# Splitting first-layer sums from SBUF, an earlier load, and product tiles in turns in a fused conditioned S4D and FFN kernel

## The chip, the cores and the metric

The kernel runs on one core of a Trainium2 chip. The metric is the device time of one execution in microseconds (us). TensorE (PE) multiplies matrices into PSUM, and PEld is its weight load. VectorE (DVE) and ScalarE (ACT) do elementwise work, GpSimd (POOL) and SyncE (SP) mostly issue DMAs here. Each engine runs its own queue of instructions in order and waits on semaphores of the others.

## The reference

```python
mod = (silu(c) @ w_mod)          # sa, ca, ga, sb, cb, gb, each of 576
h = layernorm(x) * (1 + ca) + sa
x = x + ga * S4D(h)              # y = h conv K + h * D_skip, by FFTs
h = layernorm(x) * (1 + cb) + sb
x = x + gb * (relu(h @ w1) @ w2) # 576 -> 4608 -> 576
...
K = 2 * Re(einsum("dn,dnl->dl", C, exp(A dt l)))   # 128 states, l < 2048
```

There are 2048 tokens of 576 channels, all float32.

## The kernel before

The tokens are worked in four blocks of 512. The convolution is done by blocks as well: `conv(s)` transforms the normed input (U) and the kernel (K) of block s (PE into `ps_f`, L757, copied by ACT to Z, L758), finishes the transforms as butterflies on DVE (L509), multiplies spectra on DVE (`product`: outputs Y, scratch T, L509), and transforms back (PE into `ps_i`, L998). The norm before the feed-forward network then makes `xh`, `xl` and `xs`, a high and low part of the normed input (L1059 to L1066). Spectra that later blocks need go to DRAM and back through POOL's DMA queue: saves of U, R and K (Ud, Rd, Kd, L748), loads of them (Ua, R, Ka, L744), and `kt` (L1238), the kernel's time samples.

The convolution kernel K itself is built by `rest`, in pieces `h`: `load` fetches W0, Zr and W2r on POOL (L398 to L400), `rot` turns W by phases on DVE into W1r (L408 to L414), and `products` multiplies W2r and W1r on PE (L440, output `kps`), in four column tiles of 32, `dd`, with 48, 32 or 16 columns by the number of blocks that the piece serves. Each float32 matmul shows as two matmul instructions in the profile. The pieces for block 1, (1, 2, 3) or 1 alone, are done first; those for blocks 2 and 3, 32 columns, are done during block 1 of the feed-forward network.

That network is the main loop, `ffn`: 36 slices of the hidden layer for each block, 144 iterations g in all. `first(g)` sums 14 matmuls of 128x512 into a PSUM tile `hps` (L1305; two buffers). ACT takes `hh` = relu of it, rounded to the high part (L1310), and DVE takes the low part `hl` from `hps` and `hh` (L1311). `second(g - 2)`, 14 more matmuls, adds into five accumulators (L1330), which ACT evacuates at a block's end (L1416; `oT` and `o`). In each iteration the weights are split as well: ACT rounds `w` (L1276 and L1283), DVE subtracts (L509, `w<-r,w`).

The rest of the work is written as Python generators that `yield` a cost (DVE work in us), `None` for a small PE piece, or -1 for a break. `step(g)` is called four times in an iteration and pulls pieces from the generator of the block, until a rate, a room or a -1 stops it. During block 0 the generator is first `rest` for block 1's pieces and then `conv(1)`; during block 1 it is `finish(0)`, `rest` for blocks 2 and 3, and `conv(2)`; and so on. A scheduler orders each engine's queue from that program order; some instructions are held to it (`kept`).

Of the kernel before, what the change touches and what calls it, by code (L numbers as in the profile page):

```python
# [10 lines left out]
F32 = mybir.dt.float32  # L11
F32R = mybir.dt.float32r
I32 = mybir.dt.int32
AF = mybir.ActivationFunctionType
# [32 lines left out]
class KGen:  # L47
# [335 lines left out]
    def rest(self, psum, items, beside=iter(())):  # L383


        nc, k = self.nc, self.k
        v = nc.vector.tensor_tensor
        kes, rows = {}, {}
        most = 16 * max(len(blocks) for _, blocks in items)
        with ExitStack() as ctx:  # L390
            pt = k.pool(ctx, f"kr{items[0][1][0]}")

            def load(h):
                W2 = pt.tile([P, 2, 32, H], F32, tag="W2", bufs=2, name=f"W2r_{h}")
                W0 = pt.tile([P, 16, 2, H], F32, tag="W0", bufs=2 if most == 48 else 1, name=f"W0_{h}")
                Z = pt.tile([P, 2, 2, H], F32, tag="Z", bufs=2, name=f"Zr_{h}")
                d = nc.gpsimd.dma_start
                d(out=W0.rearrange("p (y a) r c -> p y (a r c)", y=2), in_=strips(k.W1d[h], 2))  # L398
                d(out=Z.rearrange("p i r c -> p (i r c)"), in_=k.Zd[h])
                k.gate = d(out=W2.rearrange("p r (y b) c -> p (r y) (b c)", y=2), in_=strips(k.W2d[h], 4))  # L400
                return W2, W0, Z

            def rot(out, X, Z, i):
                cb = [P, 32, H]
                flat = "p a r c -> p (a r) c"
                T = pt.tile([P, 16, 2, H], F32, tag="T", name="T")
                zr, zi = (Z[:, i, r].unsqueeze(1).broadcast_to(cb) for r in range(2))
                v(T.rearrange(flat), X.rearrange(flat), zi, op=ALU.mult)  # L408
                yield 1.75
                v(out.rearrange(flat), X.rearrange(flat), zr, op=ALU.mult)  # L410
                yield 1.75
                v(out[:, :, 0], out[:, :, 0], T[:, :, 1], op=ALU.subtract)  # L412
                yield 0.95
                v(out[:, :, 1], out[:, :, 1], T[:, :, 0], op=ALU.add)  # L414
                yield 0.95

            def rots(W1, W0, Z, blocks):
                a = [W1[:, 16 * i : 16 * i + 16] for i in range(len(blocks))]
                if blocks[0] == 1:
                    yield from rot(a[0], W0, Z, 0)  # L420
                    if len(blocks) > 1:
                        yield from rot(a[1], W0, Z, 1)
                        yield from rot(a[2], a[0], Z, 1)
                else:
                    yield from rot(a[0], W0, Z, 1)
                    yield from rot(a[1], a[0], Z, 0)

            def products(h, W1, W2, blocks):
                na = 16 * len(blocks)
                key = (h // 6, blocks)  # L430
                if key not in kes:
                    kes[key] = pt.tile([P, na, 72], F32, name=f"ker_{h}")
                ke = kes[key]
                for half in range(2):
                    ps = psum.tile([P, 6, na], F32, tag="cps", bufs=1, name="kps")
                    for q in range(6):
                        for dd in range(4):
                            ch = dd * 12 + 6 * half + q
                            for r in range(2):
                                nc.tensor.matmul(  # L440
                                    ps[32 * dd : 32 * dd + 32, q, :],
                                    W2[:, r, :, ch],
                                    W1[:, :na, r, ch],
                                    start=(r == 0),
                                    stop=(r == 1),
                                )
                        if q == 2:
                            yield None
                    q0 = 12 * (h % 6) + 6 * half
                    nc.scalar.activation(  # L450
                        ke[:, :, q0 : q0 + 6], ps.rearrange("p q a -> p a q"), AF.Copy
                    )
                    yield None
                rows[key] = rows.get(key, 0) + 1
                if rows[key] == 6:
                    yield -1
                    for i, s in enumerate(blocks):
                        self.store(
                            s, h // 6, ke[:, 16 * i : 16 * i + 16].rearrange("p a q -> p (a q)"),
                            nc.gpsimd,  # L460
                        )

            nxt = load(items[0][0])
            yield -1
            prev = iter(())
            for i, (h, blocks) in enumerate(items):
                W2, W0, Z = nxt
                W1 = pt.tile([P, most, 2, H], F32, tag="W1", bufs=2, name=f"W1r_{h}")
                yield from spread(rots(W1, W0, Z, blocks), prev, len(blocks))
                if i + 1 < len(items):  # L470
                    nxt = load(items[i + 1][0])
                prev = products(h, W1, W2, blocks)
                if i + 2 == len(items):
                    yield next(beside, -1)
            yield from both(prev, beside)
# [11 lines left out]
class Body:  # L487
# [317 lines left out]

    def norms(self, st, kept):

        nc = self.nc
        rs = []
        for i in range(4):  # L810
            mv = self.sm.tile([P, 5], F32, tag="mv", bufs=4, name="mv")
            nc.vector.bn_aggr(out=mv[:, 0:2], in_=st[i])
            sq = nc.scalar.activation(mv[:, 2:3], mv[:, 1:2], AF.Sqrt, bias=self.eps)
            if kept:
                self.tc.keep_in_program_order(sq)
            else:
                self.kept(sq)
            rs.append(mv)
        for mv in rs:
            nc.vector.reciprocal(mv[:, 3:4], mv[:, 2:3])  # L820
            nc.vector.tensor_scalar(
                mv[:, 4:5], mv[:, 0:1], mv[:, 3:4], -1.0, op0=ALU.mult, op1=ALU.mult
            )
        return rs

    def sums(self, name):
        return [self.sm.tile([P, 2, 6], F32, tag="st", bufs=8, name=name) for _ in range(4)]
# [11 lines left out]
    def norm1(self, x2, h):  # L839

        f = self.nc.vector.scalar_tensor_tensor
        st = self.sums("st1")
        for p in range(2):
            yield from self.stats(
                lambda i: x2[:, i, p * PC : (p + 1) * PC], [t[:, p] for t in st]
            )
        rs = self.norms(st, False)
        yield 2.0
        for i in range(4):
            mv = rs[i]  # L850
            f(h[:, i], x2[:, i], mv[:, 0:1], self.m["ca"], op0=ALU.subtract, op1=ALU.mult)
            f(h[:, i], h[:, i], mv[:, 3:4], self.m["sa"], op0=ALU.mult, op1=ALU.add)
            yield 1.6

    def conv(self, s):
# [33 lines left out]
        def spec_K(p, Z):  # L889
            R = self.load(self.Rd[s - 1][p], "R")  # L890
            Rs.append(R)
            K = self.spec(f"K_{s}_{p}")
            yield from self.butterfly(Z, K, -1)
            yield -1
            if s + 1 < NB:
                self.save(self.Rd[s][p], K)
            f = nc.vector.scalar_tensor_tensor
            K2 = self.spec(f"K2_{s}_{p}")
            f(K2[:, :, 0], R[:, :, 1], self.sgn[:, 1:2], K[:, :, 0], op0=ALU.mult, op1=ALU.add)
            yield 1.35  # L900
            f(K2[:, :, 1], R[:, :, 0], self.sgn[:, 0:1], K[:, :, 1], op0=ALU.mult, op1=ALU.add)
            yield 1.35
            yield -1
            if s + 1 < NB:
                self.save(self.Kd[s][p], K2)
            Ks.append(K2)

        def product(p, Y):
            def pair(t):
                if t == 0 or s == 1:  # L910
                    Ka = (Rs if t else Ks)[p]
                else:
                    Ka = self.load(self.Kd[s - t][p], "Ka")
                Ua = Us[p] if t == s else self.load(self.Ud[t][p], "Ua")
                return Ka, Ua

            order = [0, s, *range(1, s)]
# [14 lines left out]
            yield from self.butterfly(Y, V, 1)  # L932
            Vs.append(V)

        Us, Ks, Rs, Vs = [], [], [], []
        if s == 1:
            ZU = self.spec("Z")
            yield from mm_U(0, ZU)
# [3 lines left out]
            yield from both(spec_U(1, Z1), mm_K(0, ZK))  # L942
            kt[1] = self.load_kt(s, 1)
            yield from spec_K(0, ZK)
            ZK = self.spec("Z")
            Y = self.spec(f"Y_{s}_0")
            yield from both(product(0, Y), mm_K(1, ZK))
        else:
            ZK = self.spec("Z")
            yield from both(self.norm1(x2, h), mm_K(0, ZK))  # L950
# [295 lines left out]
    def ffn(self, gens):  # L1246
# [50 lines left out]
        def first(g):  # L1297
# [9 lines left out]
                    step(g)  # L1307
            hh = ff.tile([P, 512], F32R, tag="hh", bufs=3, name="hh")
            hl = ff.tile([P, 512], F32R, tag="hl", bufs=3, name="hl")
            nc.scalar.activation(hh, ps, AF.Relu)  # L1310
            nc.vector.scalar_tensor_tensor(hl, ps, 0.0, hh, op0=ALU.max, op1=ALU.subtract)  # L1311
            return hh, hl

        def second(g, hh, hl):
# [246 lines left out]
```

## Time and profile before

| | |
|---|---|
| time, median of 3 runs | 1366.92 us (1363.95 to 1371.61) |
| profiled execution, span | 1360.4 us |
| PE busy | 1226.0 us, 90% |
| DVE busy | 871.4 us, 64% |
| ACT busy | 503.5 us, 37% |
| POOL busy | 195.3 us, 14% |

For the profiled execution only the span of its records is known; it lies 6.5 us under the median of the timed runs. Start times in the profile are counted from the start of that span. Feed-forward work begins at about 213 us; block 0 ends near 551, block 1 lasts from 559 to 849, block 2 to 1110, and block 3 to 1342. A row of a timeline has start, duration, engine, line, operation, output and inputs, shape, and in brackets the idle time before it and what ended that.

### The profile page before, as it was taken

What the parts mean: (1) busy time and instruction counts of PE and PEld (TensorE: products, weight loads), DVE (VectorE), ACT (ScalarE), POOL (GpSimd) and SP (SyncE); (2) the same over time, 40 slices, a digit from 0 to 9 for tenths busy, and PEclk for the clock granted to TensorE, in tenths of its full rate; (3) what the DMA queues carried; (4) which work ended last, traced back from release to release, by engine and by line L of the source; (5) the groups of instructions that cost most, each with busy time, mean ns of one, the idle gap of its engine ahead of it and who ended that gap; (6) DMA issues with size and microseconds to landing.
All of it is one profiled execution on the core that took longest, in us unless ns stands there. A gap on an engine that the chain in (4) does not pass through costs nothing.

```text
span 1360.4 us, 26053 instructions
## 1 busy us (share of the span) xinstructions
PE 1226.0 (90%) x10608; PEld 973.7 (72%) x10608; DVE 871.4 (64%) x1351; ACT 503.5 (37%) x1014; POOL 195.3 (14%) x271
## 2 busy tenths in 40 slices
PE   5125797999999987999999999999999999999998
PEld 3124565777787766777777887787888888888886
DVE  5978997998878698469737986266999222111111
ACT  7986234222224311622233225333322253233321
POOL 1777231111120100021101100100010000000000
PEclk9557899999999998999999999999999999999999
DMA  6666499988898755699689894677997567666651
GB/s 196 243 246 241 135 356 366 331 292 275 292 344 289 265 199 207 205 362 316 236 278 342 294 362 143 206 245 233 317 348 259 178 177 211 198 195 197 197 174 61
DMA packets 132424, 340.47 MB, mean 250 GB/s; under 512 B 22352, under 2 KB 22672, under 8 KB 132304
## 3 DMA queue, kind: packets, MB, share of 16 engines
q1 hardware_dynamic: 105200, 215.21, 48.9%
q0 software_dynamic: 26816, 123.01, 24.6%
q8 instruction: 83, 1.36, 0.4%
q10 hardware_dynamic: 288, 0.59, 0.1%
q14 instruction: 37, 0.30, 0.1%
HBM read 258.55 MB, written 80.22 MB: 249 GB/s over the span
## 4 chain that ended last, share of the span: by engine, by line
PE 70%; DVE 11%; DMA 10%; issue 4%; ACT 2%; POOL 1%; SPq 0%; DVEq 0%; ACTq 0%; POOLq 0%
PE acc L1330 28%; PE hps L1305 28%; PE kps L440 5%; PE ps_f L757 4%; PE kps L262 3%; DVE T L509 2%; DVE Y L509 2%; DMA Ua<-Ud 2%; DMA Ud<-U 2%; DVE k L133 1%; PE ps_i L998 1%; DMA h<-in_x_dram 1%; DMA Ka<-Rd 1%; DMA Zr<-Zd 1%; DMA W1d<-W 1%
## 5 line engine op out<-in xcount | busy, mean ns | idle before, releaser
L1330 PE MATMUL acc<-hh,w 128*128 128x512 f32 x1296 | 422.1, 400 | 0.3 <-DVE w L509 0.3
L1305 PE MATMUL hps<-xh,w 128*128 128x512 f32 x1152 | 394.3, 402 | 4.4 <-ACT xh L1061 3.5
L1311 DVE SCALAR_TENSOR_TENSOR hl<-hps,hh 128x512 fp32r<-128x512 f32 x144 | 99.0, 688 | 291.3 <-ACT hh L1310 291.0
L1330 PEld LDWEIGHTS acc<-hh,w 128*128 128x128 f32 x1296 | 242.1, 188 | 52.5 <-DVE w L509 0.9
L1330 PE MATMUL acc<-hl,w 128*128 128x512 f32 x720 | 278.7, 399 | 0.0
L1305 PEld LDWEIGHTS hps<-xh,w 128*128 128x128 f32 x1152 | 217.4, 190 | 52.1 <-ACT xh L1061 4.7
L1305 PE MATMUL hps<-xl,w 128*128 128x512 f32 x576 | 230.8, 401 | 0.2 <-DVE xl L1066 0.2
L1310 ACT ACTIVATE hh<-hps 128x512 fp32r<-128x512 f32 x144 | 86.0, 598 | 354.6 <-PE hps L1305 347.0
L1283 ACT ACTIVATE w<-r 128x576 fp32r<-128x576 f32 x144 | 98.6, 686 | 217.9 <-issue 168.4
L1330 PEld LDWEIGHTS acc<-hl,w 128*128 128x128 f32 x720 | 135.3, 188 | 28.2
L1305 PEld LDWEIGHTS hps<-xl,w 128*128 128x128 f32 x576 | 109.2, 190 | 24.8 <-DVE xl L1066 1.5
L1305 PE MATMUL hps<-xs,w 128*128 128x512 f32 x288 | 97.2, 417 | 14.3 <-DVE hl L1311 14.0
L1276 ACT ACTIVATE w<-r 128x640 fp32r<-128x640 f32 x142 | 104.0, 733 | 12.4 <-DMA r<-in_w_dram 12.4
L262 PE MATMUL kps<-W,W 128*32 128x16 f32 x2304 | 40.3, 215 | 71.5 <-POOL W L59 47.3
L262 PEld LDWEIGHTS kps<-W,W 128*32 128x32 f32 x2304 | 37.9, 150 | 76.2 <-POOL W L59 49.7
L440 PEld LDWEIGHTS kps<-W1r,W2r 128*32 128x32 f32 x3456 | 68.4, 146 | 30.7 <-issue 16.8
L509 DVE TENSOR_TENSOR Y<-Y,T 128x1152 f32<-128x1152 f32 x64 | 84.7, 1351 | 0.2
L440 PE MATMUL kps<-W1r,W2r 128*32 128x48 f32 (+2 forms) x3456 | 77.4, 238 | 7.0 <-DVE W1r L412 3.3
L1305 PEld LDWEIGHTS hps<-xs,w 128*128 128x128 f32 x288 | 52.8, 190 | 28.3 <-DVE hl L1311 17.1
L758 ACT ACTIVATE Z<-ps_f 128x288 f32<-128x288 f32 x104 | 42.4, 407 | 63.1 <-PE ps_f L757 62.3
L509 DVE TENSOR_TENSOR w<-r,w 128x512 fp32r<-128x512 f32 (+2 forms) x108 | 57.9, 572 | 8.6 <-ACT w L1283 8.6
L509 DVE TENSOR_TENSOR W<-Z 128x576 f32<-128x576 f32 x52 | 37.1, 752 | 29.3 <-ACT Z L758 29.3
(216 smaller groups left out, 1362.8 us busy)
## 6 DMA issues: line engine op xcount, KB each, us to landing
r<-in_w_dram SPq DMA_DIRECT2D x144, 320.0 KB, 4.2
r<-in_w_dram SPq DMA_DIRECT2D x144, 288.0 KB, 3.7
w<-L1d SPq DMA_DIRECT2D x108, 320.0 KB, 3.0
w<-L2d SPq DMA_DIRECT2D x108, 288.0 KB, 3.2
W2r<-W2d POOLq DMA_DIRECT2D x18, 1536.0 KB, 9.4
W2d<-W SPq DMA_DIRECT2D x10, 1536.0 KB, 7.4
W<-W1d POOLq DMA_DIRECT2D x18, 768.0 KB, 8.9
Ua<-Ud POOLq DMA_DIRECT2D x12, 1152.0 KB, 10.3
```

The lines of the kernel that those rows point to most:

```text
L133: self.nc.vector.scalar_tensor_tensor(f[:, i].rearrange(pair, u=2), th, float(slot), k[:, i].rearrange(pair, u=2), op0=ALU.mult, op1=ALU.s ...
L262: self.nc.tensor.matmul(ps[32 * dd : 32 * dd + 32, 12 * u + q, :], W2[:, r, :, ch], W1[:, u, :, r, ch], start=(r == 0), stop=(r == 1),)
L440: nc.tensor.matmul(ps[32 * dd : 32 * dd + 32, q, :], W2[:, r, :, ch], W1[:, :na, r, ch], start=(r == 0), stop=(r == 1),)
L509: return self.kept(self.nc.vector.tensor_tensor(*args, **kw))
L757: kept(nc.tensor.matmul(o, fc[:, n2, c, :], src(n2), start=True, stop=True))
L758: nc.scalar.activation(Z[:, n2, c], ps[:, :PC], AF.Copy)
L1276: nc.scalar.activation(w[:, 0], r, AF.Copy)
L1283: nc.scalar.activation(w[:, 0:D], r2[g], AF.Copy)
L1305: nc.tensor.matmul(ps, a, x, start=(i == 0), stop=(i == 13))
L1310: nc.scalar.activation(hh, ps, AF.Relu)
L1311: nc.vector.scalar_tensor_tensor(hl, ps, 0.0, hh, op0=ALU.max, op1=ALU.subtract)
L1330: nc.tensor.matmul(acc[i], a, x, start=(f == 0 and j in (0, 3, 6, 9, 12)), stop=(f == NF - 1 and j in (2, 5, 8, 11, 13)),)
```

## The change

1. `first`: ACT writes the relu of `hps` to a new float32 tile `raw` in SBUF; ACT copies `raw` to `hh`; DVE subtracts `raw - hh`. Only ACT's first operation reads `hps`.
2. `norms` is cut into `roots` and `factors`; the norm ahead of a convolution breaks off for three steps between them.
3. In `conv(1)` the load of Ua is issued between the two halves of K's butterfly, not in `product`; Y gets its buffer before Z, and the second half's transform of K begins three pieces later.
4. `rest` for blocks 2 and 3 breaks off five times in place of once after its first load.
5. In `products` the loop over real and imaginary part, r, stands outside that over the column tile, dd: consecutive matmuls go to different tiles.
6. The memory for DMA descriptors is set to 8192 bytes.

```diff
-                        for dd in range(4):
-                            ch = dd * 12 + 6 * half + q
-                            for r in range(2):
+                        for r in range(2):
+                            for dd in range(4):
+                                ch = dd * 12 + 6 * half + q
                                 nc.tensor.matmul(
...
             nxt = load(items[0][0])
-            yield -1
+            for _ in range(1 if most == 48 else 5):
+                yield -1
...
-        rs = self.norms(st, False)
-        yield 2.0
+        rs = self.roots(st, False)
+        yield 1.0
+        for _ in range(3):
+            yield -1
+        self.factors(rs)
+        yield 1.0
...
             K = self.spec(f"K_{s}_{p}")
-            yield from self.butterfly(Z, K, -1)
+            W = self.spec("W")
+            yield from self.butterfly1(Z, W)
+            if s == 1:
+                Uas.append(self.load(self.Ud[0][p], "Ua"))
+            yield from self.butterfly2(W, K, -1)
...
+            Y = self.spec(f"Y_{s}_0")
             ZK = self.spec("Z")
-            Y = self.spec(f"Y_{s}_0")
-            yield from both(product(0, Y), mm_K(1, ZK))
+            yield from both(product(0, Y), after(3, mm_K(1, ZK)))
...
-            nc.scalar.activation(hh, ps, AF.Relu)
-            nc.vector.scalar_tensor_tensor(hl, ps, 0.0, hh, op0=ALU.max, op1=ALU.subtract)
+            raw = ff.tile([P, 512], F32, tag="raw", bufs=2, name="raw")
+            nc.scalar.activation(raw, ps, AF.Relu)
+            nc.scalar.activation(hh, raw, AF.Copy)
+            nc.vector.tensor_tensor(hl, raw, hh, op=ALU.subtract)
...
-    nc = bacc.Bacc("TRN2", target_bir_lowering=False, num_devices=1)
+    nc = bacc.Bacc("TRN2", target_bir_lowering=False, num_devices=1, dynamic_dma_scratch_size=8192)
```

The added lines shift later ones: L744 and L748 become L745 and L749, L1238 becomes L1259, L1305 becomes L1326, L1310 becomes L1332 (`raw`) and L1333 (`hh`), L1311 becomes L1334, L1330 becomes L1353, L1416 becomes L1439.

How the order of instructions changes is shown at three places. The first is POOL's queue in `conv(1)`, before (a DMA's tile has its number; Ud_0_101 and Ud_1_102 are block 0's spectra, the two halves):

```order
L748 DMA Ud_0_103<-U_0_5378 128x4x576
L744 DMA R<-Rd_0_109 128x4x576
L748 DMA Ud_1_104<-U_1_5469 128x4x576
L1238 DMA kt<-kd_1_60 128x16x72
L748 DMA Rd_0_111<-K_0_5563 128x4x576
L748 DMA Kd_0_115<-K_1_0_5615 128x4x576
L744 DMA Ua<-Ud_0_101 128x4x576
L744 DMA R<-Rd_1_110 128x4x576
L748 DMA Rd_1_112<-K_1_5846 128x4x576
L744 DMA Ua<-Ud_1_102 128x4x576
```

And after:

```order
L749 DMA Ud_0_103<-U_0_5436 128x4x576
L745 DMA R<-Rd_0_109 128x4x576
L749 DMA Ud_1_104<-U_1_5542 128x4x576
L745 DMA Ua<-Ud_0_101 128x4x576
L1259 DMA kt<-kd_1_60 128x16x72
L749 DMA Rd_0_111<-K_0_5645 128x4x576
L749 DMA Kd_0_115<-K_1_0_5694 128x4x576
L745 DMA R<-Rd_1_110 128x4x576
L745 DMA Ua<-Ud_1_102 128x4x576
L749 DMA Rd_1_112<-K_1_5923 128x4x576
```

The first Ua moves ahead of kt, Rd and Kd, the second ahead of one Rd.

The second place is the change from block 0 to block 1. On PE, before (acc_0 are block 0's accumulators; xs_6182 and xh_6180 are block 1's input):

```order
L1330 MATMUL acc_0_3035<-hh,w_6324 128x512 x2
L1330 MATMUL acc_0_3035<-hl,w_6324 128x512
L1305 MATMUL hps<-xs_6182,w_6162 128x512 x2
L1305 MATMUL hps<-xs_6182,w_6262 128x512 x2
L1330 MATMUL acc_0_3036<-hh,w_6324 128x512
L1049 MATMUL ps_t<-ident,h_0_6241 128x128 x2
L1049 MATMUL ps_t<-ident,h_1_6242 128x128 x2
L1330 MATMUL acc_0_3036<-hh,w_6324 128x512
```

And after:

```order
L1353 MATMUL acc_0_3044<-hh,w_6385 128x512 x2
L1353 MATMUL acc_0_3044<-hl,w_6385 128x512
L1353 MATMUL acc_0_3045<-hh,w_6385 128x512
L1353 MATMUL acc_0_3045<-hl,w_6385 128x512
L1326 MATMUL hps<-xs_6257,w_6223 128x512 x2
L1326 MATMUL hps<-xs_6257,w_6322 128x512 x2
L1070 MATMUL ps_t<-ident,h_0_6324 128x128 x2
L1070 MATMUL ps_t<-ident,h_1_6325 128x128 x2
```

Block 0's last sums now all stand ahead of block 1's first matmul. On ACT at the same place, before:

```order
L1059 ACTIVATE xf<-ps_t,m_sb,m_cb 128x512
L1416 ACTIVATE oT<-acc_0_3035,m_gb 128x512
L1061 ACTIVATE xh_6180<-xf 128x512
L1059 ACTIVATE xf<-ps_t,m_sb,m_cb 128x512
L1416 ACTIVATE oT<-acc_0_3036,m_gb 128x512
L1061 ACTIVATE xh_6180<-xf 128x512
L1059 ACTIVATE xf<-ps_t,m_sb,m_cb 128x512
L1061 ACTIVATE xh_6180<-xf 128x512
L1059 ACTIVATE xf<-ps_t,m_sb,m_cb 128x512
L1061 ACTIVATE xh_6180<-xf 128x512
L1310 ACTIVATE hh<-hps 128x512
L1276 ACTIVATE w_6392<-r_6364 128x640
```

And after:

```order
L1439 ACTIVATE o_6528<-acc_0_3045,m_gb 128x512
L1082 ACTIVATE xh_6255<-xf 128x512
L1080 ACTIVATE xf<-ps_t,m_sb,m_cb 128x512
L1304 ACTIVATE w_6546<-r_6438 128x576
L1082 ACTIVATE xh_6255<-xf 128x512
L1080 ACTIVATE xf<-ps_t,m_sb,m_cb 128x512
L1082 ACTIVATE xh_6255<-xf 128x512
L1332 ACTIVATE raw<-hps 128x512
L1297 ACTIVATE w_6466<-r_6436 128x640
L1333 ACTIVATE hh<-raw 128x512
L1332 ACTIVATE raw<-hps 128x512
L1297 ACTIVATE w_6511<-r_6482 128x640
```

The evacuations of the accumulators all stand ahead of the third xh now (the four oT just above these rows), and a weight split stands between `raw` and `hh`.

The third place is the first piece of `rest` in block 1. On PE before, the products follow the sums of block 1's sixth slice (weights w_6503):

```order
L1305 MATMUL hps<-xl_6181,w_6503 128x512
L1305 MATMUL hps<-xh_6180,w_6503 128x512
L440 MATMUL kps<-W1r_6585,W2r_6566 32x32
L1330 MATMUL acc_36_6515<-hh,w_6550 128x512 x2
L1330 MATMUL acc_36_6515<-hl,w_6550 128x512
L440 MATMUL kps<-W1r_6585,W2r_6566 32x32 x47
```

And after, behind those of the seventh (w_6663):

```order
L1326 MATMUL hps<-xl_6256,w_6663 128x512
L1326 MATMUL hps<-xh_6255,w_6663 128x512
L440 MATMUL kps<-W1r_6710,W2r_6644 32x32 x48
L1353 MATMUL acc_36_6593<-hh,w_6683 128x512 x2
L1353 MATMUL acc_36_6593<-hl,w_6683 128x512
```

The products stand one iteration later against the sums; on DVE the rotations that make W1r follow the same number of `hl`s (40) as before.

More of the change, by code (lines that the diff above doesn't have):

```diff
@@ L806, in norms, with roots @@
     def norms(self, st, kept):
+        rs = self.roots(st, kept)
+        self.factors(rs)
+        return rs
+    def roots(self, st, kept):
         nc = self.nc
@@ L818, in norms, with factors @@
             rs.append(mv)
+        return rs
+    def factors(self, rs):
+        nc = self.nc
         for mv in rs:
@@ L823, in norms @@
             )
-        return rs
     def sums(self, name):
@@ L846, in norm1 @@
             )
-        rs = self.norms(st, False)
-        yield 2.0
+        rs = self.roots(st, False)
+        yield 1.0
+        for _ in range(3):
+            yield -1
+        self.factors(rs)
+        yield 1.0
         for i in range(4):
@@ L913, in pair @@
                     Ka = self.load(self.Kd[s - t][p], "Ka")
-                Ua = Us[p] if t == s else self.load(self.Ud[t][p], "Ua")
+                if t == s:
+                    return Ka, Us[p]
+                Ua = Uas[p] if s == 1 else self.load(self.Ud[t][p], "Ua")
                 return Ka, Ua
@@ L933, in back @@
             Vs.append(V)
-        Us, Ks, Rs, Vs = [], [], [], []
+        Us, Ks, Rs, Vs, Uas = [], [], [], [], []
         if s == 1:
```

## The prediction

> **What bounds the kernel now.** I read the page first, then the stage table, the waits, and the timelines of the stages in which TensorE (PE) is not full. The page's first section and its chain:
>
> ```profile
> PE 1226.0 (90%) x10608; PEld 973.7 (72%) x10608; DVE 871.4 (64%) x1351; ACT 503.5 (37%) x1014; POOL 195.3 (14%) x271
> ...
> PE 70%; DVE 11%; DMA 10%; issue 4%; ACT 2%; POOL 1%; SPq 0%; DVEq 0%; ACTq 0%; POOLq 0%
> ```
>
> PE is the bound on average, but DVE and DMA hold a fifth of the chain. The stage table (span from : to, its length, then busy time per engine) says where:
>
> ```profile
> core 0: us, PE busy (x) PEld busy (x) DVE busy (x) ACT busy (x) POOL busy (x), PEclk, DMA share, GB/s
> ...
> 245.00:345.00 100.00, 97.93 (x1741) 78.04 (x1731) 94.22 (x100) 23.51 (x44) 14.09 (x21) 1.00 0.85 297
> 345.00:483.00 138.00, 136.29 (x1306) 105.43 (x1305) 107.21 (x156) 44.93 (x91) 18.59 (x27) 1.00 0.80 279
> 483.00:541.00 58.00, 45.29 (x174) 34.69 (x173) 55.11 (x79) 9.70 (x16) 3.00 (x4) 0.92 0.64 223
> 541.00:594.00 53.00, 53.00 (x247) 41.54 (x247) 23.69 (x52) 27.32 (x48) 6.20 (x10) 0.99 0.74 249
> 594.00:603.00 9.00, 5.72 (x109) 4.37 (x108) 6.41 (x7) 1.57 (x3) 1.31 (x2) 0.84 1.03 394
> 603.00:852.00 249.00, 245.21 (x2018) 193.56 (x2018) 186.23 (x239) 85.11 (x159) 25.30 (x34) 1.00 0.82 284
> ```
>
> From 483 to 541 PE idles 12.7 us and the granted clock is 0.92, which is 58 x 0.08 = 4.6 us more; DVE is busy 55.11 of 58, so DVE sets the pace there. From 594 to 603 there are 3.3 us of idle and 9 x 0.16 = 1.4 us of clock. Elsewhere after 245 PE is at least 97% busy. The PE timeline shows what it waits for (in brackets the idle time before, and its releaser):
>
> ```profile
> 524.95 1.22 PE L1305 MATMUL hps<-xs,w 128*128 128x512 f32 x2 [4.81 <-DVE hl L1311]
> ...
> 536.04 1.22 PE L1305 MATMUL hps<-xs,w 128*128 128x512 f32 x2 [2.81 <-DVE hl L1311]
> ...
> 598.50 0.31 PE L440 MATMUL kps<-W1r,W2r 128*32 128x32 f32 x2 [3.28 <-DVE W1r L412]
> ```
>
> First-layer sums wait for `hl`, because both `hps` buffers are full until DVE has read them, and DVE's queue is late. Why DVE is late, and (second fence) what POOL does before that:
>
> ```profile
> 466.45 2.63 DVE L509 TENSOR_TENSOR Y<-K,Ua 128x1152 f32<-128x1152 f32 x2 [5.01 <-DMA Ua<-Ud]
> ...
> 512.05 2.63 DVE L509 TENSOR_TENSOR Y<-K,Ua 128x1152 f32<-128x1152 f32 x2 [2.79 <-DMA Ua<-Ud]
> ```
>
> ```profile
> 440.73 0.76 POOL L748 DMA_DIRECT2D Ud<-U  x1 [8.96 <-DVE U L509]
> ...
> 454.82 0.76 POOL L748 DMA_DIRECT2D Kd<-K  x1 [2.49 <-DVE K L901]
> 455.57 0.75 POOL L744 DMA_DIRECT2D Ua<-Ud  x1
> ...
> 501.06 0.75 POOL L744 DMA_DIRECT2D Ua<-Ud  x1
> ```
>
> Each Ua is issued behind the saves of K's results and lands 10.9 us later (455.57 to 466.45), while DVE stands idle for 5.01 and 2.79 us.
>
> **The change, part by part.**
>
> *Ua behind the butterfly's first half.* The first Ua now stands right behind the save of Ud on POOL, so it can be issued near 441.5 and land near 452.5, 14 us ahead of its use; the three DMAs moved behind it (kt, Rd, Kd) go 0.75 us later each, and each of them waits longer for its producer than that. The second stands ahead of Rd and Kd but waits for the buffer of the half before; it is issued perhaps 5 us sooner. Both waits go: 5.01 + 2.79 = 7.8 us off DVE's queue, which sets the end of this stage. I take 7.8. The lower end is 3 (only the later Ua is near the stalls, and the queue of DVE has other waits); the upper is 14, when the freed `hps` lets PE hold one more first layer ahead as well (14 matmuls, 3.2 us at 0.23 us each, the step between two rows at 547 below) and the lost clock returns. Late next is DVE's own work.
>
> *Sums split from SBUF.* The rows for the three forms, and for the same kind of split from SBUF in the norm:
>
> ```profile
> L1310 ACT ACTIVATE hh<-hps 128x512 fp32r<-128x512 f32 x144 | 86.0, 598 | 354.6 <-PE hps L1305 347.0 <-DVE x L509 4.7 <-DVE Y L509 2.4
> ...
> L1311 DVE SCALAR_TENSOR_TENSOR hl<-hps,hh 128x512 fp32r<-128x512 f32 x144 | 99.0, 688 | 291.3 <-ACT hh L1310 291.0
> ...
> L1061 ACT ACTIVATE xh<-xf 128x512 fp32r<-128x512 f32 x16 | 10.1, 631 | 5.0 <-DMA W1d<-W 4.3 <-DVE xf L1057 0.3
> ...
> L1066 DVE TENSOR_TENSOR xl<-xf,xh 128x512 fp32r<-128x512 f32 x16 | 11.1, 692 | 19.0 <-ACT xh L1061 18.9
> ```
>
> ACT gets 144 x 0.631 = 91 us more, 37% becoming 44%; DVE's `hl` costs the same (692 against 688 ns). `hps` comes free after ACT's `raw`, not after DVE: that is what removes the `hl` stalls of PE. `hh` comes 0.63 us later, or about 1.3 with the weight split that the order puts between; `second` uses it two iterations (about 12 us) later, so in steady state this costs nothing, the cover being that distance. The place without cover is the start of block 1:
>
> ```profile
> 547.07 0.39 PE L1305 MATMUL hps<-xl,w 128*128 128x512 f32 x1
> 547.30 0.40 PE L1305 MATMUL hps<-xh,w 128*128 128x512 f32 x1
> 547.53 1.13 PE L998 MATMUL ps_i<-V,gc 128*128 128x288 f32 x4
> ...
> 558.74 1.07 PE L1305 MATMUL hps<-xs,w 128*128 128x512 f32 x4
> ```
>
> ```profile
> 557.84 0.69 DVE L1064 TENSOR_TENSOR xs<-xf,xs 64x512 fp32r<-64x512 f32 x1 [1.21 <-ACT xs L1061]
> ```
>
> ```profile
> L1416 ACT ACTIVATE oT<-acc,m_gb 128x512 f32<-128x512 f32 x12 | 7.5, 690 | 0.0
> ```
>
> The first matmul of block 1 (558.74) starts as xs is ready (558.53), with 17 acc matmuls left behind it as filler. Now these stand ahead, and ACT evacuates all five accumulators among xf, xs and xh, where two stood before: three more of about 0.69 us, 2.1, and 0.6 for hh: I take a loss of 2.5 (1 to 8; 8 if PE also sits out the 9.9 us from the last ps_i, 548.66, to xs with 33 matmuls, 7.6 us, to do meanwhile, and waits for each xh, with clock lost on top).
>
> The Trainium skill ("VectorE: DVE Perf Modes", section "Rules for kernel authors") advises, for elementwise work on a matmul's output, to accept the PSUM source or to copy to SBUF first only where many operations follow; here one follows, which speaks against this edit. The rows agree that the operation itself gains nothing (692 against 688 ns), but the rule does not count when the PSUM buffer is given back. By it alone the edit only lengthens the way to `hl`, and what that gives here is rival 1's result, with its chance.
>
> *Products four steps on.* PE's products of block 1 stand one iteration (28 matmuls, 6.3 us) later, while the rotations on DVE keep their place among the `hl`s. That covers the 3.28 us and most of the clock behind it: 4.5 of 3.3 + 1.4 (0 to 4.7; 0 if DVE's rotations slip as far). DVE's wait for Zr stays beside PE:
>
> ```profile
> 588.22 1.76 DVE L408 TENSOR_TENSOR T<-W,Zr 128x1536 f32<-128x1536 f32 x1 [4.34 <-DMA Zr<-Zd]
> ```
>
> *Product tiles in turns.* 3456 small matmuls, on one column tile four in a row now; the nearest rows:
>
> ```profile
> 189.52 0.75 PE L632 MATMUL mps_sb<-wm_sb,cb 128*32 128x128 f32 x20
> ...
> 247.75 2.33 PE L440 MATMUL kps<-W1r,W2r 128*32 128x48 f32 x96
> ...
> 252.93 1.64 PE L440 MATMUL kps<-W1r,W2r 128*32 128x16 f32 x94
> ...
> 638.54 0.95 PE L440 MATMUL kps<-W1r,W2r 128*32 128x32 f32 x48
> ```
>
> Start to start, taking off one duration (266, 212 and 235 ns by the grouped rows): 48 columns (2330 - 266) / 95 = 21.7 ns, 16 columns 15.4, 32 columns 15.2. L632 already goes over its tiles in turns, and does 128 columns in (750 - 276) / 19 = 24.9 ns, hardly more than 48 on one tile: turns do overlap. Bounds: nothing at one end; at the other, all scale as L632 does (128 columns on one tile would be 58 by the 48-column rate, so a factor 0.43): 21.7 to 9.3 and 15.3 to 6.6. Between, I take 15.4 for 48 columns, a rate that the rows show, and 2 ns off the others. 48 columns: 1152 x 6.3 = 7.3 us, but most of them lie from 245 to 345, where DVE has only 5.8 us to spare; I take 4. The others, in stages where PE is full: by the table of L440's own rows
>
> ```profile
> 345.00:483.00 138.00, 19.20 (x816) 16.95 (x816) 1.00 0.80 279
> ...
> 603.00:852.00 249.00, 20.93 (x1056) 18.44 (x1056) 1.00 0.82 284
> ```
>
> (816 + 1056) x 2 ns = 3.7. Together 7.5 (0 to 5.8 + 1872 x 8.7 ns = 22).
>
> The Trainium skill ("TensorEngine Tiling (Array Packing)", section "Instruction Overhead") gives each matmul some 60 cycles, so that few columns cost the same as 60: by that alone turns bring nothing, which is rival 3's result. The rows speak against it as a floor for every instruction: 48 and 16 columns differ, 21.7 against 15.4 ns. No run here shows the floor in turns yet.
>
> *Norm factors behind the roots.*
>
> ```profile
> 407.11 0.54 DVE L820 RECIPROCAL mv<-mv 128x1 f32<-128x1 f32 x3 [5.46 <-ACT mv L813]
> ```
>
> DVE stops waiting 5.46 us for the roots, but in that stage PE is busy 136.29 of 138: 0, hidden by PE (up to 1.7). *Smaller scratch for DMA descriptors*: few POOL transfers are in flight together: 0, no row can price it.
>
> **The sum.** 7.8 - 2.5 + 4.5 + 7.5 = 17.3 us off the span of 1360.4, so 1343.1. The median of the runs, 1366.9, lies 6.5 above the profiled span, and what lies around the span does not change: 1366.9 - 17.3 = 1349.6, in round numbers 1350.
>
> **Rivals.** (1) Slower: `hl` stands at the head of DVE's queue while `hh` is now 1.3 us later, and where DVE is the pace that is lost each time. In the stages where DVE is over 90% busy, 245 to 345 and 483 to 541, and in as much again of the start and of 426 to 483, some 18 iterations are so placed: 23 us, with the Ua gain gone and 12 from turns and products kept: 1366.9 + 23 - 12 = 1378. It decides if DVE reaches `hl` less than 1.3 us behind the sums, as it did here:
>
> ```profile
> 456.27 0.69 DVE L1311 SCALAR_TENSOR_TENSOR hl<-hps,hh 128x512 fp32r<-128x512 f32 x1 [0.27 <-ACT hh L1310]
> ```
>
> Against it: sums that are no longer held by `hl` come earlier against DVE's queue. 8%.
> (2) The Ua gain is eaten at block 1's start, since xs and the xh are one chain through ACT: loss 8 instead of 2.5, and turns bring half: 1349.6 + 5.5 + 3.75 = 1359. 17%. (3) The turns bring nothing, a fixed cost per matmul: 1357. 13%. (4) The turns reach L632's factor for all: 22 instead of 7.5, 1335. 15%. The forecast itself 47%.
>
> A measurement of this kernel tells about 0.5%, 6.8 us, from no change. Faster by more (under 1360.1) holds the forecast, (3), (4) and half of (2): 0.78 with some kept for what is not listed; same 0.14; slower 0.08. The range reaches from (4) to a little beyond (2): 1334 to 1364.
>
> **What would show it.** In the changed trace no `Y<-K,Ua` waits for Ua, and PE's idle time between 470 and 541 falls from about 13 to below 5 us with a clock of 1.0; `hl` releases no PE matmul any more. At block 1's start PE idles some 2 to 3 us at xs or xh. The 3.28 us before L440 are gone. Runs of 96 products with 48 columns take about 1.75 us in place of 2.33. If `hl` waits for `hh` where DVE is full, rival 1; if the idle at xs is above 6 us, rival 2; if 2.33 stays, rival 3. The forecast is wrong in sign only if the longer way to `hh` holds up DVE's queue.

## The result, and the profile after

The changed kernel takes 1350.91 us (median of 6 runs, 1348.6 to 1353.41) against 1367.59 for the kernel before in the same runs: ratio 0.9896, 95% interval 0.987 to 0.9923, so some 14 us (11 to 18). The forecast was 1350, that is 17.3 us less. The time came out; several terms of the sum did not, and they are what can be learned from. The two profiled executions, from which everything below is read, differ by 11.1 us (spans 1360.4 and 1349.3).

The page of the changed kernel, first section and chain:

```profile
span 1349.3 us, 26128 instructions
...
PE 1219.7 (90%) x10608; PEld 970.2 (72%) x10608; DVE 870.7 (65%) x1351; ACT 579.4 (43%) x1158; POOL 195.2 (14%) x271
...
PE 72%; DVE 11%; DMA 8%; issue 4%; ACT 3%; POOL 1%; SPq 0%; DVEq 0%; POOLq 0%; ACTq 0%
```

ACT is busy for 76 us more, DVE for as long as before, and DMA has less of the chain. The stage table, cut within 0.4 us of the first matmul of each block's first layer:

```profile
214.00:543.50 329.50, 317.55 (x3418) 249.43 (x3416) 291.19 (x391) 121.85 (x229) 41.00 (x60) 0.98 0.84 297
543.50:834.50 291.00, 284.08 (x2278) 224.09 (x2278) 204.13 (x262) 116.81 (x218) 32.79 (x46) 0.99 0.81 285
834.50:1102.00 267.50, 263.70 (x1157) 210.98 (x1156) 166.11 (x233) 118.33 (x213) 14.60 (x20) 0.99 0.71 241
```

and the same of the kernel before:

```profile
212.60:558.70 346.10, 324.26 (x3405) 251.90 (x3406) 291.03 (x390) 100.41 (x190) 40.98 (x60) 0.98 0.80 280
558.70:852.50 293.80, 286.73 (x2297) 226.15 (x2297) 207.42 (x265) 103.64 (x190) 32.81 (x46) 0.99 0.82 285
852.50:1113.00 260.50, 260.45 (x1148) 209.72 (x1147) 163.12 (x229) 95.95 (x171) 14.57 (x20) 1.00 0.76 247
```

Block 0 is 17 us shorter, block 1 is 3 us shorter, and block 2 is 7 us longer, which nothing in the prediction said. Block 0 first. In its last stretch this is all that DVE waited for before (from 456 us to the `xs` of block 1; each line has the total in us, how often, and the longest):

```profile
DVE Y L509 <- DMA Ua<-Ud: 7.8, 2, 5.0
DVE hl L1311 <- ACT hh L1310: 4.5, 2, 4.2
DVE x L509 <- PE ps_i L998: 3.2, 2, 3.1
DVE w L509 <- ACT w L1283: 2.9, 1, 2.9
DVE xs L1064 <- ACT xs L1061: 1.2, 1, 1.2
```

and after (from 455 us to the same point):

```profile
DVE xs L1085 <- ACT xs L1082: 5.1, 1, 5.1
DVE x L510 <- PE ps_i L1019: 0.2, 1, 0.2
```

19.6 us of waiting became 5.3: 14.3 us, and the stretch from the `hl` at 456.3 (455.4 after) to xs went from 101.6 to 87.4 us. The two differences agree, so the waits explain the stretch; only the one for `xs` grew. Ua lands in time, as the POOL and DVE timelines of the changed kernel show:

```profile
440.91 0.76 POOL L745 DMA_DIRECT2D Ua<-Ud  x1
...
482.47 0.75 POOL L745 DMA_DIRECT2D Ua<-Ud  x1 [4.50 <-DVE W L510]
```

```profile
456.01 2.63 DVE L510 TENSOR_TENSOR Y<-K,Ua 128x1152 f32<-128x1152 f32 x2
...
499.17 1.35 DVE L510 TENSOR_TENSOR Y<-K,Ua 128x1152 f32<-128x1152 f32 x1
```

No bracket stands behind the two products, so neither waited. The stage in which PE idled 12.7 us before, at a granted clock of 0.92 (483 to 541), is now

```profile
483.00:534.00 51.00, 48.53 (x207) 38.48 (x206) 50.72 (x81) 16.19 (x27) 1.74 (x3) 1.00 0.71 249
```

with 2.5 us of idle time and a clock of 1.00. No sum waits for `hl` there any more; the stalls that are left are for the weights' low part, which DVE makes as well:

```profile
518.38 1.82 PE L1353 MATMUL acc<-hh,w 128*128 128x512 f32 x5 [1.29 <-DVE w L510]
...
527.21 1.82 PE L1353 MATMUL acc<-hh,w 128*128 128x512 f32 x5 [0.98 <-DVE w L510]
```

Now block 2. PE's one long wait there, and ACT and DVE before it:

```profile
875.48 0.75 PE L758 MATMUL ps_f<-kt,fcK 128*128 128x288 f32 x2 [3.79 <-ACT Z L759]
```

```profile
869.77 0.41 ACT L759 ACTIVATE Z<-ps_f 128x288 f32<-128x288 f32 x1 [0.84 <-PE ps_f L758]
874.28 0.85 ACT L820 ACTIVATE mv<-mv,eps 128x1 f32<-128x1 f32 x4 [4.10 <-DVE mv L819]
875.04 0.39 ACT L759 ACTIVATE Z<-ps_f 128x288 f32<-128x288 f32 x1
```

```profile
871.16 2.98 DVE L804 BATCH_NORM_STATS2 st<-x 128x6 f32<-128x288 f32 x8 [6.84 <-DMA x<-in_x_dram]
```

The roots of the norm for block 3 stand in ACT's queue while x, its input, is still under way; the copy of `ps_f` behind them waits, and PE, out of buffers, waits for that copy. Before, ACT waited for the same roots (3.0 us), but one Z copy stood behind them where two stand now (first the order before, then after):

```
L758 ACTIVATE Z<-ps_f 128x288 x3
L813 ACTIVATE mv<-mv,eps 128x1 x4
L758 ACTIVATE Z<-ps_f 128x288
```

```
L759 ACTIVATE Z<-ps_f 128x288 x3
L820 ACTIVATE mv<-mv,eps 128x1 x4
L759 ACTIVATE Z<-ps_f 128x288 x2
```

### The profile page after: what moved, and what is told of

Same layout as the page of the kernel before. It is cut to its first block, busy times and chain, and to the rows that moved or that the text cites. A ratio compares the mean times of both kernels' runs of the same rounds, so it can differ in the third digit from the quotient of the medians.

```text
span 1349.3 us, 26128 instructions
## 1 busy us (share of the span) xinstructions
PE 1219.7 (90%) x10608; PEld 970.2 (72%) x10608; DVE 870.7 (65%) x1351; ACT 579.4 (43%) x1158; POOL 195.2 (14%) x271
## 4 chain that ended last, share of the span: by engine, by line
PE 72%; DVE 11%; DMA 8%; issue 4%; ACT 3%; POOL 1%; SPq 0%; DVEq 0%; POOLq 0%; ACTq 0%
PE hps L1326 29%; PE acc L1353 29%; PE kps L440 5%; PE ps_f L758 4%; PE kps L262 3%; DVE T L510 2%; DVE Y L510 1%; DMA Ud<-U 1%; DMA x<-in_x_dram 1%; PE ps_i L1019 1%; DVE k L133 1%; DMA r<-in_w_dram 1%; DMA Zr<-Zd 1%; DVE W L510 1%; DMA W1d<-W 1%
## 5 line engine op out<-in xcount | busy, mean ns | idle before, releaser
L1353 PE MATMUL acc<-hh,w 128*128 128x512 f32 x1296 | 425.7, 400 | 2.5 <-DVE w L510 2.3
L1326 PE MATMUL hps<-xh,w 128*128 128x512 f32 x1152 | 394.3, 402 | 2.8 <-ACT xh L1082 2.8
L1334 DVE TENSOR_TENSOR hl<-raw,hh 128x512 fp32r<-128x512 f32 x144 | 99.4, 690 | 290.7 <-ACT hh L1333 287.9
L1353 PE MATMUL acc<-hl,w 128*128 128x512 f32 x720 | 284.3, 401 | 0.0
L1353 PEld LDWEIGHTS acc<-hh,w 128*128 128x128 f32 x1296 | 243.9, 189 | 55.3 <-DVE w L510 4.0
L1326 PEld LDWEIGHTS hps<-xh,w 128*128 128x128 f32 x1152 | 216.6, 189 | 50.4 <-ACT xh L1082 4.2
L1326 PE MATMUL hps<-xl,w 128*128 128x512 f32 x576 | 230.6, 400 | 0.1
L1332 ACT ACTIVATE raw<-hps 128x512 f32<-128x512 f32 x144 | 86.1, 598 | 322.4 <-PE hps L1326 316.2
L1353 PEld LDWEIGHTS acc<-hl,w 128*128 128x128 f32 x720 | 136.1, 189 | 28.5
L1326 PEld LDWEIGHTS hps<-xl,w 128*128 128x128 f32 x576 | 109.0, 189 | 25.0 <-DVE xl L1087 1.9
L1326 PE MATMUL hps<-xs,w 128*128 128x512 f32 x288 | 99.4, 413 | 0.3 <-DVE xs L1085 0.3
L1333 ACT ACTIVATE hh<-raw 128x512 fp32r<-128x512 f32 x144 | 89.7, 623 | 0.3
L440 PEld LDWEIGHTS kps<-W1r,W2r 128*32 128x32 f32 x3456 | 64.1, 146 | 31.0 <-issue 19.5
L440 PE MATMUL kps<-W1r,W2r 128*32 128x48 f32 (+2 forms) x3456 | 72.3, 238 | 9.3 <-issue 5.9
L1326 PEld LDWEIGHTS hps<-xs,w 128*128 128x128 f32 x288 | 53.6, 190 | 12.6 <-DVE xs L1085 0.9
```

Source lines behind the costliest of these rows:

```text
L440: nc.tensor.matmul(ps[32 * dd : 32 * dd + 32, q, :], W2[:, r, :, ch], W1[:, :na, r, ch], start=(r == 0), stop=(r == 1),)
L1326: nc.tensor.matmul(ps, a, x, start=(i == 0), stop=(i == 13))
L1332: nc.scalar.activation(raw, ps, AF.Relu)
L1333: nc.scalar.activation(hh, raw, AF.Copy)
L1334: nc.vector.tensor_tensor(hl, raw, hh, op=ALU.subtract)
L1353: nc.tensor.matmul(acc[i], a, x, start=(f == 0 and j in (0, 3, 6, 9, 12)), stop=(f == NF - 1 and j in (2, 5, 8, 11, 13)),)
```

## The experiments

After the first trace the theory was that DVE's queue sets the end of block 0, with Ua its main wait (theory 1); the rival was that the `hps` buffers, freed late, set it, so that the split alone would do (rival 2). The stage lengths below, in us, are of one profiled execution each, between the first matmuls of the first layers. They scatter: the changed kernel and "conv(3) later" have the same order on PE in blocks 0 and 1, and differ there by 2 and 3 us. So 2 to 3 us in one of these blocks can be chance. What lies ahead of block 0 differs by up to 6 us between these executions and is left out. Each ratio is to the kernel before, run beside it.

| kernel | ratio to before (95%) | block 0 | block 1 | block 2 |
|---|---|---|---|---|
| before | 1 | 346.1 | 293.7 | 260.8 |
| split alone | 0.9995 (0.9976 to 1.0013) | 344.6 | 292.7 | 267.3 |
| Ua alone | 0.9896 (0.9849 to 0.9943) | 336.3 | 295.6 | 261.0 |
| turns alone | 0.9977 (0.9953 to 1.0) | 344.1 | 294.2 | 261.0 |
| factors alone | 0.9967 (0.9947 to 0.9987) | 344.0 | 292.8 | 261.3 |
| changed kernel | 0.9896 (0.987 to 0.9923) | 329.1 | 291.0 | 267.7 |
| without the split | 0.9888 (0.9864 to 0.9913) | 336.1 | 287.4 | 262.3 |
| without Ua | 0.9968 (0.9949 to 0.9988) | 339.2 | 287.5 | 268.9 |
| without factors | 0.9919 (0.9888 to 0.9949) | 334.5 | 292.7 | 269.2 |
| without steps | 0.9933 (0.9913 to 0.9953) | 329.8 | 292.0 | 268.4 |
| conv(3) later | 0.9878 (0.9862 to 0.9895) | 327.1 | 287.6 | 267.7 |

**The split alone** (and the descriptor memory, which makes room for `raw`):

```diff
-            nc.scalar.activation(hh, ps, AF.Relu)
-            nc.vector.scalar_tensor_tensor(hl, ps, 0.0, hh, op0=ALU.max, op1=ALU.subtract)
+            nc.scalar.activation(raw, ps, AF.Relu)
+            nc.scalar.activation(hh, raw, AF.Copy)
+            nc.vector.tensor_tensor(hl, raw, hh, op=ALU.subtract)
```

> The kernel before with the split from SBUF alone (and the smaller descriptor memory that makes room for raw). Theory 1: the end of block 0 is set by DVE's queue, whose waits for Ua (5.0 and 2.8 us) stay; the sums no longer wait for hl, so the waits of DVE on ps_i and on hh near 545 to 556 (3.1 and 4.2 us) shrink. First matmul of block 1 about 5 us sooner than before (558.7), time about 1361 to 1363. Rival 2: the stalls of the sums on hl set the end, and freeing hps is enough: first matmul of block 1 at 545 or sooner, time about 1353.

No difference, 0.9995. The sums no longer wait for `hl`, but PE now waits for the weights' low part on the same late queue, and DVE for Ua as before:

```profile
524.35 0.80 PE L1305 MATMUL hps<-xs,w 128*128 128x512 f32 x1 [4.18 <-DVE w L509]
```

```profile
468.76 2.63 DVE L509 TENSOR_TENSOR Y<-K,Ua 128x1152 f32<-128x1152 f32 x2 [6.02 <-DMA Ua<-Ud]
...
514.59 2.63 DVE L509 TENSOR_TENSOR Y<-K,Ua 128x1152 f32<-128x1152 f32 x2 [2.80 <-DMA Ua<-Ud]
```

Rival 2 falls: freeing `hps` is not enough. Theory 1 missed as well: it had the first matmul of block 1 some 5 us sooner, but block 0 is 1.5 us shorter, within the scatter, and block 2 is 6.5 us longer. The smaller descriptor memory is in this run too; it was not run alone.

**Ua alone**:

```diff
-            yield from self.butterfly(Z, K, -1)
+            yield from self.butterfly1(Z, W)
+            if s == 1:
+                Uas.append(self.load(self.Ud[0][p], "Ua"))
+            yield from self.butterfly2(W, K, -1)
...
-            yield from both(product(0, Y), mm_K(1, ZK))
+            yield from both(product(0, Y), after(3, mm_K(1, ZK)))
```

> The kernel before with Ua's early load alone. Theory 1: DVE's 7.8 us of waiting for Ua go and the end of block 0 comes 7 to 8 us sooner, time about 1359; the sums still wait for hl. Rival 2: hps stays coupled to DVE, so what DVE gains shows as other waits; less than 3 us, 1364 or more.

The ratio is 0.9896, and block 0 is 9.8 us shorter. The ratio is that of the whole change, but its interval is wide (0.5% to 1.5%), so theory 1's 8 us agree with it too; by the traces the three blocks are 7.7 us shorter here and 12.9 in the changed kernel. Rival 2 is out. From the same `hl` on (466.0) to xs (554.2) DVE now takes 88.2 us. It waits for no Ua, and its wait for `hh` fell with that from 4.5 to 0.5 us:

```profile
DVE w L509 <- ACT w L1289: 3.9, 1, 3.9
DVE x L509 <- PE ps_i L1004: 2.7, 4, 1.4
DVE hl L1317 <- ACT hh L1316: 0.5, 1, 0.5
DVE mv L820 <- ACT mv L813: 0.3, 1, 0.3
```

That is 7.4 us in place of 19.6: the early load alone takes 12.2 us of waiting off this stretch, not 7.8.

**The turns alone**:

```diff
-                        for dd in range(4):
-                            for r in range(2):
+                        for r in range(2):
+                            for dd in range(4):
```

> The kernel before with the product tiles in turns alone. From the changed trace: 48 columns 21.6 ns start to start against 22.2, 32 and 16 columns 14.9 against 15.5, so 3456 x 0.65 = 2.2 us of PE time, of which 1 to 2 us show: 1365 to 1366. If the prediction's 7.5 us were there but hidden by something else in the whole change, 1359 to 1361.

The ratio is 0.9977, 3 us with an interval from 0 to 6: near the 2.2 us that the rows give, and the prediction's 7.5 are out.

**The changed kernel without the factors' new place**:

```diff
-        rs = self.roots(st, False)
-        yield 1.0
-        for _ in range(3):
-            yield -1
-        self.factors(rs)
-        yield 1.0
+        rs = self.norms(st, False)
+        yield 2.0
```

> The changed kernel with the norm's roots and factors together again. If the factors' place is what makes PE wait 3.8 us for a copy of Z near 871 us (block 2 is 7 us longer than before), that wait is gone and the time is about 1345; block 0 is at most 1 to 2 us longer, since DVE's wait for the roots fell only from 5.5 to 4.3 us. If the wait near 871 comes from the split or from the order alone, it stays, and the time is 1351 to 1353.

The wait in block 2 stays (4.34 us, same place, 269.2 us in all): it is not the factors' doing. Block 0 is 5.4 us longer, which neither theory expected. **The factors alone** on the kernel before were run for this:

> The kernel before with the norm factors three steps behind the roots alone. The prediction gave this nothing, as PE is full there. If that holds, within 2 us of before. If DVE's queue carries it to the end of block 0 (the changed kernel without it is 5 us longer in block 0), 1362 or less; Ua's late load may still hide it.

The ratio is 0.9967, 4.5 us, interval 2 to 7: it is not nothing. In its one profiled execution block 0 is 2.1 and block 1 0.9 us shorter, which is no more than the scatter. DVE's wait for the roots itself hardly falls (5.5 to 4.3 us in the changed kernel), so most of it probably comes by the order that follows from the later factors; this is not shown, and which instruction carries it is open.

**The changed kernel without the split**, the first diff backwards: `hh` and `hl` from `ps` again.

> The changed kernel with hl taken from PSUM again (one ACT operation instead of two). Theory 1: Ua's early load keeps most of the gain at the end of block 0; the sums wait for hl again (some 5 to 10 us between 480 and 545); time about 1355 to 1358. Rival 2: without the freed hps nearly all of the gain in block 0 is gone, time 1362 or more.

Neither came: 0.9888, as fast as the changed kernel. Block 0 is 7.0 us longer, with a sum that waits for `hl` again (1.41 us at 529.98), but block 2 is 5.4 us shorter and block 1 3.5, which can be scatter. In the table every kernel with the split takes 267 to 269 us for block 2, and every one without it 261 to 262. In all six of the table with the split PE waits there for a Z copy, 3.6 to 4.8 us. The row

```profile
890.73 0.75 PE L757 MATMUL ps_f<-kt,fcK 128*128 128x288 f32 x2 [4.07 <-ACT Z L758]
```

is that of the split alone (its line numbers are nearly those of before); in the kernel before, with Ua alone and without the split no such row exists. ACT's order goes with it: in all six with the split two Z copies stand behind the roots, in the five others one. The lateness of x does not decide it: without the split ACT takes the roots 40.2 us after the block's start, in the changed kernel 39.8, and only the latter has the wait on PE.

**The changed kernel without Ua's early load**, the second diff backwards:

> The changed kernel with Ua loaded in the product again. Theory 1: DVE waits 5 to 8 us for Ua again and the end of block 0 comes as much later, time about 1357 to 1359. Rival 2: PE runs ahead of DVE with the freed hps, the wait of DVE is beside it, and the time stays within 2 us of the changed kernel's 1351.

The ratio is 0.9968, so 10 us of the 14 are gone: theory 1's cause, and more than its 6 to 8 us. DVE waits for Ua again:

```profile
464.08 2.63 DVE L510 TENSOR_TENSOR Y<-K,Ua 128x1152 f32<-128x1152 f32 x2 [5.54 <-DMA Ua<-Ud]
```

**The changed kernel without the four steps**:

```diff
-            for _ in range(1 if most == 48 else 5):
-                yield -1
+            yield -1
```

> The changed kernel with the products of block 1 at their old step. The prediction gave the steps 4.5 us; the trace of the changed kernel shows 2.1 + 0.5 us of waiting and the lower clock once more, at the second piece. If the stall only moved: within 2 us of 1351. If the steps hold what the prediction said: 1354 to 1356.

The ratio is 0.9933 against 0.9896, about 5 us, but the intervals overlap (0.9913 to 0.9953, 0.987 to 0.9923), and in the traces only 2.5 us lie in the three blocks. With the steps PE waits at the second piece, without them at the first and less at the second ("issue" means that the profile shows nothing that PE waited for):

```profile
598.42 0.33 PE L440 MATMUL kps<-W1r,W2r 128*32 128x32 f32 x8 [2.05 <-issue]
599.24 0.82 PE L440 MATMUL kps<-W1r,W2r 128*32 128x32 f32 x40 [0.49 <-DVE W1r L414]
```

is the changed kernel, and without the steps:

```profile
584.25 0.33 PE L440 MATMUL kps<-W1r,W2r 128*32 128x32 f32 x8 [2.31 <-DVE W1r L412]
...
600.25 0.33 PE L440 MATMUL kps<-W1r,W2r 128*32 128x32 f32 x8 [1.08 <-ACT w L1303]
```

The sums are 2.5 against 3.4 us: the stall mostly moved. What the steps are worth lies between 1 and 5 us and stays open.

**Why the turns bring so little: other data for the products.**

```diff
-    W2[:, r, :, ch], W1[:, :na, r, ch]
+    # first half of a piece: moving columns side by side
+    W2[:, r, :, ch], flat_W1[:, na * j : na * j + na]
+    # second half: weights side by side
+    flat_W2[:, 32 * ch : 32 * ch + 32], W1[:, :na, r, ch]
```

> The changed kernel, whose products read other data: in the first half of each piece the moving columns lie side by side in SBUF (instead of 96 words apart), in the second half the weights do; so the convolution kernel K that it builds for blocks 1 to 3 is not the reference's. If the strided read of the moving columns is what sets 21.6 and 14.9 ns, the first halves fall to some 10 ns for 48 columns and 7 to 10 for the others; if the load of 32 strided weight columns sets it, the second halves do. If each product has a fixed cost of its own, neither changes.

Runs of products, moving columns side by side (L449) and weights side by side (L451):

```profile
291.77 1.38 PE L449 MATMUL kps<-W1r,W2r 128*32 128x48 f32 x80
...
300.56 2.23 PE L451 MATMUL kps<-W1r,W2r 128*32 128x48 f32 x96
...
307.70 0.87 PE L449 MATMUL kps<-W1r,W2r 128*32 128x16 f32 x48
...
310.44 0.61 PE L451 MATMUL kps<-W1r,W2r 128*32 128x16 f32 x48
```

In the changed kernel such a run of 48 columns is

```profile
250.00 2.31 PE L440 MATMUL kps<-W1r,W2r 128*32 128x48 f32 x96 [1.17 <-ACT ker L450]
```

Start to start, in ns, in a typical run of each kind: 48 columns 14.7 with the columns side by side, 20.7 with the weights side by side, 21.6 in the changed kernel; 32 columns 14.4, 13.8 and 14.9; 16 columns 14.3, 9.0 and 14.8. So a product of 48 columns is held by its strided columns, one of 16 by its 32 strided weights, and at 32 the two are nearly alike. No fixed cost holds 16 columns at 14.8; whether one sets the 9.0 that is left, no run shows. In this kernel neighbouring products also share columns, or weights. For the columns the next run, in which they share none, settles that; for the weights it stays open. The span is 1337.3 us, of one execution alone.

**Columns side by side, with the right result**: W1r as (r, channel, column), which the rotations then write with a stride.

```diff
-    W1 = pt.tile([P, most, 2, H], F32, tag="W1", bufs=2, name=f"W1r_{h}")
+    W1 = pt.tile([P, 2, H, most], F32, tag="W1", bufs=2, name=f"W1r_{h}")
...
-    W1[:, :na, r, ch],
+    W1[:, r, ch, :na],
```

> The changed kernel with W1r laid out so that the moving columns of a product lie side by side, as a change that keeps the result (the rotations on DVE then write and read with a stride). If strided reads of the moving columns set the rate, 48 columns take 14.7 instead of 21.6 ns, 8 us of PE in block 0, and the time falls by 6 to 9 us; if the strided rotations cost DVE more than 1.75 us each, block 0 gets longer instead, since DVE is nearly full there.

It is much slower, 1.0489 (1.0461 to 1.0517): block 0 takes 379.6 us. DVE's rotations are what pays; DVE is busy for 972.6 us in place of 870.7:

```profile
L409 DVE TENSOR_TENSOR W1r<-W,Zr 128x1536 f32<-128x1536 f32 x24 | 71.0, 2980 | 0.0
L411 DVE TENSOR_TENSOR W1r<-W1r,T 128x768 f32<-128x768 f32 x36 | 58.6, 1629 | 0.1
```

for 1757 and 956 ns in the changed kernel. The products do go faster, 14.7 ns in the first of these two rows, but most of them run as in the second, at 19.7:

```profile
257.48 1.61 PE L439 MATMUL kps<-W1r,W2r 128*32 128x48 f32 x96
...
329.74 2.15 PE L439 MATMUL kps<-W1r,W2r 128*32 128x48 f32 x96
```

The granted clock is 1.00 in the first and 0.50 in the second, where PE has been waiting for DVE. Strided columns show no such difference: the changed kernel's run at 245.32, at a clock of 0.50, takes 21.6 ns as well. The Trainium skill ("SBUF — State Buffer", section "Door 1: The DMA port swizzle (why `[64,N]` ≈ `[32,N]`)") says that each access which crosses to a new 16-byte line of SBUF pays a penalty. These runs agree in kind, on PE's reads and on DVE: 21.6 against 14.7 ns, 2980 against 1757. At which stride the penalty begins, no run here shows.

**conv(3) four steps later**, to let x land before the roots:

```diff
-        yield -1
-        yield -1
+        for _ in range(6 if s == 3 else 2):
+            yield -1
```

> The changed kernel with conv(3) begun four steps later, so that x has landed when ACT takes the roots in block 2. If the 6 to 8 us that block 2 loses in every kernel with the split come from the roots standing ahead of Z copies on ACT while x is still under way, PE's wait for Z is gone and block 2 takes 261 instead of 267.7 us: ratio to before about 0.985, 1345 to 1347. If the split's longer work on ACT costs it in another way, block 2 stays at 267 and the time at 1351.

This missed: block 2 stays at 267.7, and PE waits 3.55 us at the same distance from the block's start. The step moved the transforms as well, and x still was late:

```profile
868.75 2.98 DVE L804 BATCH_NORM_STATS2 st<-x 128x6 f32<-128x288 f32 x8 [6.65 <-DMA x<-in_x_dram]
```

Its load waits until the output of block 1 has left the same buffer (POOL waited 3.3 us for out_dram), so the start of `conv` does not set it. The time, 0.9878, cannot be told from the changed kernel's. **Both, the layout and conv(3) later:**

> The changed kernel with both: conv(3) four steps later and W1r laid out with its columns side by side. If the two add up, 6 us of block 2 and 8 us of block 0 go: ratio to before about 0.979, some 1338 us. If DVE's rotations suffer from the stride, 1345 or more.

The ratio is 1.0479 (1.0456 to 1.0501), as with the layout alone. No version beat the changed kernel by more than the measurement tells.

## Why the prediction was right, and where its steps were not

- **Bound and place: right.** The kernel without Ua's load (0.9968) and Ua's load alone (0.9896) show that the end of block 0 hung on DVE's queue and on this wait.
- **Ua, 7.8 us, and the loss of 2.5 at block 1's start: too small by 10 together.** The first matmul of block 1 came 15.2 us sooner (558.7 to 543.5), where 5.3 were forecast. The step that failed is that of DVE's queue: it counted the Ua waits alone, while the waits for `hh`, `ps_i` and the weights, 10.6 us, stood in the same stretch and went too. With Ua alone block 0 is 9.8 us shorter; the split, the factors and the turns, each alone, give 1.5 to 2.1, within the scatter. Together the four make 15.4 of the 17.0 us. Taken out of the changed kernel, the factors cost block 0 5.4 us and the split 7.0, so the parts help each other, and no share can be given to each. The lower clock of PE is gone as well (0.92 from 483 to 541 before, 1.00 from 483 to 534). At block 1's start PE had no idle time over 0.5 us. DVE's wait for ACT's part of xs grew from 1.2 to 5.1 us, but PE had work in its queue until xs was ready at 543.46, so rival 2's place did not cost.
- **The split, 0 in steady state: wrong in a place not looked at.** Beside the other parts it takes 7.0 us from block 0 and gives 5.4 back in block 2, where the order on ACT changed. That it is worth nothing here is shown (0.9888 without it), not that it must be. The prediction asked who waits for `hh`, but not what else in ACT's queue changes place.
- **Turns, 7.5 us: two to three times too much.** Some 0.6 ns of 22.2 and of 15.5 were saved on each product, 2.2 us in all, and 3 (0 to 6) measured. The step that failed took L632's rate and the 16-column rate as what four tiles can reach; L632 reads its columns side by side, and the products don't. The sum also took 384 products of 48 columns twice, once in the 4 us and once among the 1872 (0.8 us). Rival 3 was nearly right in size but not in its reason: 16 columns go at 9.0 ns once the weights lie side by side, so no fixed cost holds them at 14.8.
- **Steps, 4.5 us**: 1 to 5, undecided. The first stall went as told; the second piece's came, which the text did not name.
- **Factors, 0: wrong**, 4.5 us alone (2 to 7). "Hidden by PE" was read from a stage with PE at 99%. But DVE, not PE, set the end of block 0, so what is saved on DVE ahead of it can count; that this is the way it came is not shown.
- **Rival 1** did not come: `hl` waits 287.9 us for `hh` in the changed kernel, 291.0 before, and not at all from 455 to 544 us.
- **The base, 1366.9: misread, without harm to the sum.** The prediction put 6.5 us around the span. Every timed run on record is only 1.7 to 1.8 us longer than its own span, so some 4.7 of the 6.5 were that execution's having been quicker than the median one.

The terms that were too small (Ua, factors) and those too large or missed (turns, block 2) nearly cancel. So the bound and the main cause were understood, but that 1350 came out to 1 us is luck: the two profiled spans differ by only 11.1 us, and the ratio gives some 14 where 17.3 were forecast.

## What to carry to other kernels

Where an engine's queue sets the end of a stage, look at all its waits in that stage, not only at the one that is being removed: here 7.8 us were removed and 12.2 went. What looks hidden by a full TensorE in an earlier stage may count too. An operation added to an engine with time to spare can still change the order of what stands beside it, and one late load whose consumer stands ahead in that queue was enough here to give the gain back. Before counting on column tiles that overlap, look at the stride of their operands, and ask who has to write them in the better layout.

## What the runs showed of the hardware

The small float32 products here are paced by strided reads, of columns and of weights apart: 48 moving columns 96 words apart take 21.6 ns and side by side 14.7; with 32 weights 48 words apart a 16-column product takes 14.8, and with the weights side by side 9.0. At a granted clock of 0.50 the strided 48 columns took 21.6 ns still, those side by side 19.7. On DVE a float32 product of 128x1536 with its output written in strides took 2980 ns instead of 1757.
